# Retention and a softplus feed-forward layer: the decay of the queries moved to the outputs of the values, opening loads each into a buffer of its own, copies and rests on GpSimd

## The chip, the cores and the metric

The kernel runs on one core of one Trainium2 chip. The metric is the time of one execution on the device in microseconds (us). Below, PE is TensorE's matmul, PEld its weight load, DVE is VectorE, ACT is ScalarE, POOL is GpSimd and SP is SyncE, whose queue issues all transfers.

## What is computed

There are 8 sequences of 576 tokens with 8 heads of 64. Each head does retention, which is attention without a softmax, with scores that decay by a head's factor per token of distance; the result, 4608 tokens by 512, goes through a feed-forward layer with 2048 hidden units and a softplus between its two products.

```python
scores = scale * np.matmul(q, k.transpose(0, 1, 3, 2))
gamma = 1.0 - 2.0 ** (-5.0 - np.arange(H, dtype=np.float32))
Dmat = np.where(rel >= 0, gamma[:, None, None] ** rel[None, :, :], 0.0)
ret = scores * Dmat[None, :, :, :]
attn_out = np.matmul(ret, v)
...
h = x @ w_in
g = np.maximum(h, 0.0) + np.log1p(np.exp(-np.abs(h)))
return g @ w_out
```

The decay from token c to token r is split into two factors: gamma^(r+1), which goes with the query r, and gamma^-(c+1), which goes with the value c.

## The kernel before

**Retention in steps.** The 4608 tokens are 36 chunks of 128. A step m is half a chunk's heads, so there are 72 steps, two to a chunk. A step has up to 32 products of 64x64 (twice as many matmul records, since each is done in two passes): `scores` does 8 products of keys and queries into the score columns of a PSUM tile (L150) and then up to 8 products of keys and values, the sums from which a chunk's state is made (L155); `values` does 8 products of masked scores and values (L204) and up to 8 of states and queries (L214). In one place of the program, `scores` of step m and `values` of step m-1 stand together. `scores_out` masks the scores on DVE (L168), makes the running states u and s on DVE (L184, L193; L181, L182 and L191 at the start of a sequence) and sx, copies of states on the other half of the partitions, on POOL (L177) and DVE (L185), and scales s on POOL (L195). `values_out` writes the result of `values` into the tile xt as a head (a cast on ACT, L229) and a rest (a subtraction on DVE, L233).

**Scaling.** `scale_next` multiplies the queries of a step by the decay on POOL (L127, 128x384), in place, and from step 9 on the values too, also on POOL (L130, 128x256). The values of steps 0 to 8 are scaled on ACT in four pieces of 128x64 (L140, `scale_values`).

**The feed-forward layer in slots.** 512 tokens are a unit; there are 9 units and 16 slices of the hidden dimension, so 144 slots. Slot i does `hidden_mm(i)` (12 matmuls 128x512, L248), then ACT and DVE make the softplus (`logs`: Abs, Exp, Ln on ACT, L256 to L258; the sum on DVE, L262; the head g by a cast on ACT, L266, and the rest on DVE, L267), and PE goes on with `output_mm(i - 1)` (12 matmuls, L280). In odd slots, up to slot 127, one retention step stands ahead of `hidden_mm`: slot 1 has scores of step 9 and values of step 8, slot 3 those of 10 and 9, and so on, for the unit that comes next. At the end of a unit four results are copied out (ACT and DVE, L288 and L290) and stored.

**Weights.** The 32 weight pieces come as 64-bit floats in three staging buffers wst and are turned into two 32-bit parts while slots 0 to 14 run: L309 and L325 on ACT, L311, L317 and L330 on DVE, the last of these writing the part that `hidden_mm` of the next slot reads.

**The opening.** Ahead of slot 0, steps 0 to 8 run alone (`AHEAD` is 9), with `values` up to step 7, since `hidden_mm(0)` needs the whole xt of unit 0. The inputs of a step are 576 KB. The raw tiles have three buffers of their own and two that later belong to g, so the loads of steps 5 to 10 wait for buffers.

**What sets the order.** The program is scheduled by hand: each engine takes its instructions in the order in which they are written, and waits in its place for what an instruction needs.

Of the kernel before, what the change touches and what calls it, by code (L numbers as in the profile page):

```python
# [7 lines left out]
F32 = mybir.dt.float32  # L8
# [27 lines left out]
SMALL = 2 * QC  # L36
NCONST = NPAIR * QC + H + NPAIR
PIECE = 512
START_WEIGHTS = 2
OPENING = 5  # L40
# [18 lines left out]
def retention_softplus_ffn(ctx: ExitStack, tc, first, others, consts, w, out):  # L59
    nc = tc.nc  # L60

    const = ctx.enter_context(tc.tile_pool(name="const", bufs=1))
    wpool = ctx.enter_context(tc.tile_pool(name="wpool", bufs=1))
    xpool = ctx.enter_context(tc.tile_pool(name="xpool", bufs=2))
    att = ctx.enter_context(tc.tile_pool(name="att", bufs=2))
    moe = ctx.enter_context(tc.tile_pool(name="moe", bufs=2))
# [3 lines left out]
    ps_h = ctx.enter_context(tc.tile_pool(name="ps_h", bufs=2, space=PSUM))  # L70
    ps_att = ctx.enter_context(tc.tile_pool(name="ps_att", bufs=1, space=PSUM))
    rawp = ctx.enter_context(tc.tile_pool(name="rawp", bufs=3))
    weight_pools = ExitStack()
    wst = weight_pools.enter_context(tc.tile_pool(name="wst", bufs=WBUFS))
    later = {}

    consts_sb = const.tile([P, NCONST], F32, name="consts_sb")
    mask = const.tile([P, HC], F32, name="mask")

    decq = [consts_sb[:, n:n + SMALL].rearrange("p (s c) -> p s c", s=2) for n in (0, NCONST - SMALL)]  # L80
    vsc, gchp = consts_sb[:, SMALL:SMALL + H], consts_sb[:, SMALL + H:SMALL + H + NPAIR]


    ws = [wpool.tile([P, 2, 2 * PIECE], F32R, name=f"w{p}") for p in range(NF)]
# [17 lines left out]
    def load_step(m):  # L102

        pool, tag = (moe, "g") if m in (3, 4, 8) else (rawp, "rawp")
        r = pool.tile([P, RAW], F32, tag=tag, name=f"raw_{tag}")
        if m == 0:
            for to, at in ((consts_sb, slice(0, SMALL + H + NPAIR)), (r, slice(0, KQ)), (r, slice(KQ, RAW)),
                           (consts_sb, slice(NCONST - SMALL, NCONST))):
                nc.sync.dma_start(to[:, at], (first if to is r else consts)[:, at])
        else:  # L110
            nc.sync.dma_start(r, others[m - 1])
        kq, kv = r[:, 0:KQ], r[:, KQ:]
# [5 lines left out]
    scaled = [0]  # L118

    def scale_next():  # L120

        m = scaled[0]
        if m not in live:
            return
        scaled[0] += 1
        q = live[m]["q"]
        nc.gpsimd.tensor_mul(q, q, decq[m % 2])  # L127
        if m >= AHEAD:
            v, f = value_scale(m)
            nc.gpsimd.tensor_mul(v, v, f.unsqueeze(2).broadcast_to([P, 4, D]))  # L130
# [372 lines left out]
```

## Time and profile before

| what | value |
|---|---|
| time, median of 3 runs | 918.75 us (917.89 to 921.36) |
| the profiled execution's own time | 918.31 us |
| its span in the profile | 916.6 us |
| PE busy | 890.4 us, 97% |
| ACT busy | 442.1 us, 48% |
| DVE busy | 375.6 us, 41% |
| POOL busy | 165.6 us, 18% |
| mean granted PE clock | 0.991 |

The span is the profiled execution from its first to its last instruction; 1.7 us lie around it. A busy share is an average over three stages: the opening, the slots in which weights are still being turned into parts, and the rest. A row of the timeline has the start, the length, the engine, the line and the operation, out<-in by the program's names and, in brackets, how long the engine had been idle and what ended that.

### The profile page before, as it was taken

The page shows a single profiled execution, that of the slowest core. Times are in us where ns is not written, and L with a number is a line of the kernel's source. Part 1 is how long each engine was busy: PE and PEld are TensorE (multiplying, and loading weights), DVE is VectorE, ACT ScalarE, POOL GpSimd, SP SyncE. Part 2 cuts the span into 40 slices and gives each one's busy share as a digit, 9 for nine tenths or more (in the row PEclk, how much of TensorE's full clock was granted, in tenths as well). Part 3 has the DMA queues.
Part 4 walks back from the last instruction along what each step waited for, and adds up shares of the span by engine and source line. Part 5 has one row for each costly group of instructions (what it writes and reads, how often), then busy time and mean ns, then how long its engine had stood idle before and what let it go on. Part 6 is the DMA issues. An engine that isn't in the chain of part 4 may idle for free.

```text
span 916.6 us, 18132 instructions
## 1 busy us (share of the span) xinstructions
PE 890.4 (97%) x7830; PEld 725.7 (79%) x7830; DVE 375.6 (41%) x745; ACT 442.1 (48%) x775; POOL 165.6 (18%) x270
## 2 busy tenths in 40 slices
PE   6699999999999999999999999999999999999998
PEld 5477778888888888888888888888888888888886
DVE  4588884333423333333333333334333333332222
ACT  5577775444444454444544454445444544444444
POOL 5322121122121111111211222111211122100000
PEclk7899999999999999999999999999999999999999
DMA  8456652111211112111211121112111131001001
GB/s 289 179 189 210 201 176 76 53 52 53 99 52 53 52 38 89 53 53 52 99 53 52 36 89 53 52 54 98 53 53 45 36 98 53 27 1 46 1 1 46
DMA packets 20671, 70.24 MB, mean 77 GB/s; under 512 B 2288, under 2 KB 2544, under 8 KB 20592
## 3 DMA queue, kind: packets, MB, share of 16 engines
q1 hardware_dynamic: 20592, 69.09, 22.7%
q8 instruction: 61, 1.00, 0.5%
q14 instruction: 18, 0.15, 0.1%
HBM read 59.64 MB, written 9.44 MB: 75 GB/s over the span
## 4 chain that ended last, share of the span: by engine, by line
PE 90%; DVE 3%; ACT 3%; DMA 2%; POOL 1%; issue 0%; SPq 0%; POOLq 0%; DVEq 0%
PE h L248 43%; PE y L280 40%; PE bank L150 3%; PE bank L214 2%; PE bank L204 2%; PE bank L155 1%; DMA raw_g<-others 1%; DVE w L330 1%; DMA raw_rawp<-others 1%; DVE ab L262 1%; ACT ab L257 1%; ACT ab L258 1%; DMA wst<-w 1%; DVE wst L317 1%; ACT w L325 0%; ACT ab L256 0%
## 5 line engine op out<-in xcount | busy, mean ns | idle before, releaser
L248 PE MATMUL h<-xt,w 128*128 128x512 f32 (+1 forms) x1740 | 426.6, 394 | 8.7 <-DVE w L330 8.6
L280 PE MATMUL y<-w,g 128*128 128x512 f32 x1728 | 414.9, 389 | 0.0
L248 PEld LDWEIGHTS h<-xt,w 128*128 128x128 f32 x1740 | 320.6, 188 | 80.4 <-DVE w L330 11.9
L280 PEld LDWEIGHTS y<-w,g 128*128 128x128 f32 x1728 | 324.3, 188 | 67.3
L262 DVE SCALAR_TENSOR_TENSOR ab<-h,ab 128x512 f32<-128x512 f32 (+1 forms) x145 | 99.7, 688 | 410.1 <-ACT ab L258 410.1
L256 ACT ACTIVATE ab<-h 128x512 f32<-128x512 f32 (+1 forms) x145 | 86.3, 595 | 299.4 <-PE h L248 298.9
L267 DVE TENSOR_TENSOR g<-ab,g 128x512 fp32r<-128x512 f32 (+1 forms) x145 | 104.8, 723 | 90.9 <-ACT g L266 89.2
L266 ACT CAST g<-ab 128x512 fp32r<-128x512 f32 (+1 forms) x145 | 89.4, 617 | 101.0 <-DVE ab L262 99.9
L127 POOL TENSOR_TENSOR raw_rawp<-raw_rawp,consts_sb 128x384 f32<-128x384 f32 x69 | 72.1, 1045 | 198.8 <-DMA raw_rawp<-others 195.6
L195 POOL TENSOR_TENSOR s<-s,consts_sb 128x128 f32<-128x128 f32 x64 | 26.1, 408 | 417.8 <-DVE s L193 368.6
L258 ACT ACTIVATE ab<-ab 128x512 f32<-128x512 f32 (+1 forms) x145 | 91.2, 629 | 4.7
L257 ACT ACTIVATE ab<-ab 128x512 f32<-128x512 f32 (+1 forms) x145 | 91.2, 629 | 4.6
L130 POOL TENSOR_TENSOR raw_rawp<-raw_rawp,consts_sb 128x256 f32<-128x256 f32 x63 | 41.7, 661 | 0.0
L229 ACT CAST xt<-bank 128x256 fp32r<-128x256 f32 x68 | 25.4, 373 | 32.8 <-PE bank L214 32.8
L150 PEld LDWEIGHTS bank<-raw_rawp 64*64 64x64 f32 x1008 | 20.4, 133 | 22.2 <-issue 22.2
L214 PE MATMUL bank<-raw_rawp,sx 64*64 64x64 f32 x472 | 27.8, 221 | 4.1 <-POOL sx L177 4.1
L204 PE MATMUL bank<-a,raw_rawp 64*64 64x64 f32 x1056 | 30.1, 221 | 1.0 <-DVE xt L233 1.0
L233 DVE TENSOR_TENSOR xt<-bank,xt 128x256 fp32r<-128x256 f32 x68 | 28.3, 416 | 6.5 <-ACT xt L229 6.3
L168 DVE TENSOR_TENSOR a<-bank,mask 128x256 f32<-128x256 f32 x63 | 26.6, 423 | 9.6 <-ACT xt L229 9.6
L150 PE MATMUL bank<-raw_rawp 64*64 64x64 f32 x1008 | 29.1, 230 | 0.0
L177 POOL COPY sx<-s 64x128 f32<-64x128 f32 x64 | 24.8, 388 | 8.8 <-PE bank L214 4.8
L155 PE MATMUL bank<-raw_rawp 64*64 64x64 f32 x888 | 25.9, 218 | 0.0
(74 smaller groups left out, 412.7 us busy)
## 6 DMA issues: line engine op xcount, KB each, us to landing
raw_rawp<-others SPq DMA_DIRECT2D x68, 576.0 KB, 4.0
wst<-w SPq DMA_DIRECT2D x32, 512.0 KB, 3.7
out<-osb SPq DMA_DIRECT2D x36, 256.0 KB, 2.4
raw_g<-others SPq DMA_DIRECT2D x3, 576.0 KB, 8.8
raw_rawp<-first SPq DMA_DIRECT2D x1, 320.0 KB, 3.4
raw_rawp<-first SPq DMA_DIRECT2D x1, 256.0 KB, 4.7
consts_sb<-consts SPq DMA_DIRECT2D x1, 198.0 KB, 2.5
consts_sb<-consts SPq DMA_DIRECT2D x1, 192.0 KB, 4.9
```

Source lines behind the costliest of these rows:

```text
L127: nc.gpsimd.tensor_mul(q, q, decq[m % 2])
L150: nc.tensor.matmul(bank[rows[t], h, SCOLS][:, part[s]], L["k"][rows[h], s, part[t]], L["q"][rows[h], s, part[t]], start=True, stop=True, s ...
L204: nc.tensor.matmul(o[t][rows[h], part[s]], L["v"][rows[t], s, rows[h]], L["a"][rows[t], h, s], start=(s == 0), stop=L["states"][t] is None ...
L214: nc.tensor.matmul(o[t][rows[h], part[s]], lhs[rows[t], s], rhs, start=False, stop=True, skip_group_check=True)
L248: nc.tensor.matmul(h, ws[p][:, a, kt * P:(kt + 1) * P], xt[:, b, kt, cols], start=(n == 0), stop=(n == 3 * NKT - 1))
L256: nc.scalar.activation(ab, h, AF.Abs)
L257: nc.scalar.activation(ab, ab, AF.Exp, scale=-1.0)
L258: nc.scalar.activation(ab, ab, AF.Ln, bias=1.0)
L262: nc.vector.scalar_tensor_tensor(ab, h, 0.0, ab, op0=ALU.max, op1=ALU.add)
L266: nc.scalar.copy(g[:, HI], ab)
L267: nc.vector.tensor_sub(g[:, LO], ab, g[:, HI].bitcast(F32))
L280: nc.tensor.matmul(y, g[:, a, at:at + P], ws[p][:, b, PIECE:], start=(p == 0 and n == 0), stop=(p == NF - 1 and n == 2))
```

## The change

- The queries are no longer scaled. The decay multiplies the output of `values` instead: `values_out` does a DVE multiplication of 128x256 into a new tile x, then the cast to the head on ACT, and then the rest, on POOL (for step 7, on DVE).
- The values of all steps are scaled on ACT (`scale_values`, four pieces). In the slots, this stands in even slots behind the cast of g: `scale_values(AHEAD + i // 2)` in slot i, for the step whose products stand at the head of slot i + 1.
- `scores` is cut in two. The sums are now `sums`, and PE does them behind `values`. `states_out` is the second half of the former `scores_out`, and comes behind `values_out`.
- The second copy into sx moves from DVE to POOL and reads u rather than PSUM.
- The inputs of steps 0 to 10 each have a buffer of their own, in the space of the second half of the weights, and those of steps 0 to 8 are issued at the start, with weight piece 0 behind step 3 and pieces 1 and 2 behind step 8. The first transfers carry the constants with them; a second copy of the constants is loaded later. From step 11 on, the raw tiles have two buffers rather than three.
- The opening matmuls that have nothing to do (`OPENING`) go from 5 to 3. PSUM tiles of the opening are arranged anew, and pools change sides.

The diff, cut to its core:

```diff
-OPENING = 5
+OPENING = 3
+NOPEN = AHEAD + 2
...
     def load_step(m):
-        pool, tag = (moe, "g") if m in (3, 4, 8) else (rawp, "rawp")
-        r = pool.tile([P, RAW], F32, tag=tag, name=f"raw_{tag}")
         if m == 0:
...
+            if m < NOPEN:
+                r = openp.tile([P, RAW], F32, name=f"raw{m}")
+            else:
+                r = rawp.tile([P, RAW], F32, tag="rawp", name="rawp")
             nc.sync.dma_start(r, others[m - 1])
...
-    def scale_next():
...
-        nc.gpsimd.tensor_mul(q, q, decq[m % 2])
-        if m >= AHEAD:
-            v, f = value_scale(m)
-            nc.gpsimd.tensor_mul(v, v, f.unsqueeze(2).broadcast_to([P, 4, D]))
...
     def scale_values(m):
-        if m < AHEAD:
-            v, f = value_scale(m)
-            for n in range(4):
-                nc.scalar.activation(v[:, n], v[:, n], AF.Copy, scale=f[:, n:n + 1])
+        if m >= NSTEP:
+            return
+        v = live[m]["v"].rearrange("p s (h d) -> p (s h) d", h=2)
+        f = constant[0][0][:, 4 * (m % 2):4 * (m % 2) + 4]
+        for n in range(4):
+            nc.scalar.activation(v[:, n], v[:, n], AF.Copy, scale=f[:, n:n + 1])
...
+    def sums(m):
...
                 if follows if t else start != HC:
-                    nc.tensor.matmul(bank[rows[h], t, TCOLS][:, part[s]], L["kp"][rows[t], s, rows[h]],
+                    nc.tensor.matmul(L["bank"][rows[h], t, TCOLS][:, part[s]], L["kp"][rows[t], s, rows[h]],
                                      L["v"][rows[t], s, rows[h]], start=True, stop=True, skip_group_check=True)
...
-                nc.vector.tensor_add(sx[rows[1]], sums[0][rows[0]], before[rows[0]])
+            nc.gpsimd.tensor_copy(sx[rows[1]], between[rows[0]])
...
-        for head, _, src in todo:
-            nc.scalar.copy(head, src)
...
-                nc.vector.tensor_sub(rest, src, head.bitcast(F32))
...
+        x = att.tile([P, 2, C], F32, tag="x", name="x")
+        nc.vector.tensor_mul(x.rearrange("p s (t c) -> p s t c", t=2),
+                             bank[:, :, VCOLS].rearrange("p t (s c) -> p s t c", s=2),
+                             constant[0][2][:, pr:pr + 2].rearrange("p s (t c) -> p s t c", t=2))
+        nc.scalar.copy(hi, x)
+        rest.tensor_sub(lo, x, hi.bitcast(F32))
...
+    first_weights = {3: (0,), 8: (1, 2)}
...
-    for m in range(5):
+    for m in range(AHEAD):
         load_step(m)
-        if m == 3:
-            load_weight(0)
+        for n in first_weights.get(m, ()):
+            load_weight(n)
...
     for i in range(NSLOT):
         m = AHEAD + (i - 1) // 2
         if i % 2 and m <= NSTEP:
...
-            scores(m, both)
-            values(m - 1, [both[:, n] for n in range(2)])
-            rest = values_out(m - 1, both)
+            scores(m, bank)
+            values(m - 1, bank)
+            sums(m)
             scores_out(m)
-            rest()
-            load_next()
-            scale_next()
+            values_out(m - 1, bank, nc.gpsimd)
+            states_out(m)
+            if NOPEN <= m + 1 < NSTEP:
+                load_step(m + 1)
...
         weight_cd(n)
         gs[i] = [softplus_split(ab)]
+        if i % 2 == 0:
+            scale_values(AHEAD + i // 2)
         weight_a(n + 1)
```

In the opening, step m of the loop now writes: scores of m, values of m-1, sums of m, `scores_out(m)`, `values_out(m - 1)`, `scale_values(m + 1)`, `states_out(m)`.

The three places in the program of which the prediction speaks, in each engine's own order. First ACT, over one odd and one even slot late in the program, before: L256 to L258 are the logs of a slot, L266 the cast of g, L229 the head of the retention result.

```order
L229 CAST xt_2703<-bank 128x2x128
L256 ACTIVATE ab<-h 128x512
L257 ACTIVATE ab<-ab 128x512
L258 ACTIVATE ab<-ab 128x512
L266 CAST g<-ab 128x512
L256 ACTIVATE ab<-h 128x512
L257 ACTIVATE ab<-ab 128x512
L258 ACTIVATE ab<-ab 128x512
L266 CAST g<-ab 128x512
L229 CAST xt_2703<-bank 128x2x128
```

And of the change, where L265 to L267 are the logs, L275 the cast of g, L147 the scaling of the values and L242 the head:

```order
L242 CAST xt_2772<-x 128x2x128
L265 ACTIVATE ab<-h 128x512
L266 ACTIVATE ab<-ab 128x512
L267 ACTIVATE ab<-ab 128x512
L275 CAST g<-ab 128x512
L265 ACTIVATE ab<-h 128x512
L266 ACTIVATE ab<-ab 128x512
L267 ACTIVATE ab<-ab 128x512
L275 CAST g<-ab 128x512
L147 ACTIVATE rawp<-rawp,consts_sb 128x64 x4
L242 CAST xt_2772<-x 128x2x128
```

Four scalings now stand behind the even slot's cast of g, ahead of the next step's head.

Second, PE at the head of an odd slot, before: the last output products of the slot ahead (L280), scores (L150), sums (L155), values (L204 and L214), and the hidden products (L248).

```order
L280 MATMUL y_1817<-w_96,g 128x512 x3
L150 MATMUL bank<-raw_rawp 64x64 x8
L155 MATMUL bank<-raw_rawp 64x64 x8
L204 MATMUL bank<-a,raw_rawp 64x64 x8
L214 MATMUL bank<-raw_rawp,s 64x64
L214 MATMUL bank<-raw_rawp,sx 64x64 x2
L214 MATMUL bank<-raw_rawp,u 64x64
L214 MATMUL bank<-raw_rawp,s 64x64
L214 MATMUL bank<-raw_rawp,sx 64x64 x2
L214 MATMUL bank<-raw_rawp,u 64x64
L248 MATMUL h<-xt_662,w_98 128x512 x12
```

And of the change, with L155 the scores, L218 and L229 the values, L168 the sums and L257 the hidden products:

```order
L155 MATMUL bank<-rawp 64x64 x8
L218 MATMUL bank<-a,rawp 64x64 x8
L229 MATMUL bank<-rawp,s 64x64
L229 MATMUL bank<-rawp,sx 64x64 x2
L229 MATMUL bank<-rawp,u 64x64
L229 MATMUL bank<-rawp,s 64x64
L229 MATMUL bank<-rawp,sx 64x64 x2
L229 MATMUL bank<-rawp,u 64x64
L168 MATMUL bank<-rawp 64x64 x8
L257 MATMUL h<-xt_1816,w_970 128x512 x12
```

The sums went from second to last place, directly ahead of the hidden products.

Third, POOL at the end of the opening, before: the scaling of queries (L127) and, from step 9 on, of values (L130), the copy into sx (L177) and the scaling of s (L195).

```order
L127 TENSOR_TENSOR raw_g<-raw_g,consts_sb 128x384
L177 COPY sx<-s 64x128
L195 TENSOR_TENSOR s<-s,consts_sb 128x128
L127 TENSOR_TENSOR raw_rawp<-raw_rawp,consts_sb 128x384
L130 TENSOR_TENSOR raw_rawp<-raw_rawp,consts_sb 128x256
L177 COPY sx<-s 64x128
L195 TENSOR_TENSOR s<-s,consts_sb 128x128
```

And of the change, with L243 the rest, L193 and L200 the two copies into sx and L210 the scaling of s:

```order
L243 TENSOR_TENSOR xt_203<-x,xt_203 128x2x128
L193 COPY sx<-s 64x128
L200 COPY sx<-u 64x128
L210 TENSOR_TENSOR s<-s,part_91 128x128
L243 TENSOR_TENSOR xt_203<-x,xt_203 128x2x128
L193 COPY sx<-s 64x128
L200 COPY sx<-u 64x128
L210 TENSOR_TENSOR s<-s,part_91 128x128
```

No instruction there reads a raw tile any more; each step has a rest and a second copy instead.

More of the change, by code (lines that the diff above doesn't have):

```diff
@@ L431, in retention_softplus_ffn @@
             weight_pools.close()
-            later["osb"] = ctx.enter_context(tc.tile_pool(name="osb", bufs=4))
+            later["osb"] = ctx.enter_context(tc.tile_pool(name="osb", bufs=4, side="right"))
         if i > 0:
@@ L485 @@
     gchp = np.broadcast_to(gch.reshape(NPAIR, 2, 1), (NPAIR, 2, D)).reshape(NPAIR, P).T
[L486 removed]
     arrays = {
[L488 removed]
+        "first": np.concatenate([kq[0], vsc, gchp, kv[0], decp], axis=1).astype(np.float32),
         "others": np.concatenate([kq[1:], kv[1:]], axis=2),
[L490 removed]
+        "consts": np.concatenate([vsc, gchp, decp], axis=1).astype(np.float32),
         "w": np.stack([w_in, w_out], axis=1),
```

180 lines of the change are left out of this document (84 added, 96 removed).

## The prediction

> **What bounds the kernel now.** I read the page first, for the share of each engine and the chain that ended last.
>
> ```profile
> PE 890.4 (97%) x7830; PEld 725.7 (79%) x7830; DVE 375.6 (41%) x745; ACT 442.1 (48%) x775; POOL 165.6 (18%) x270
> ...
> PE 90%; DVE 3%; ACT 3%; DMA 2%; POOL 1%; issue 0%; SPq 0%; POOLq 0%; DVEq 0%
> ```
>
> PE is busy 97% of the span and is 90% of the chain. What is left for a change to win lies at the start; what it can lose is any wait that it puts into PE's order. The busy times by stage say where.
>
> ```profile
> 68.00:101.00 33.00, 30.79 (x254) 24.19 (x248) 29.05 (x55) 24.48 (x43) 7.77 (x11) 1.00 0.60 203
> ...
> 135.00:440.00 305.00, 305.00 (x2713) 248.85 (x2714) 111.68 (x227) 137.74 (x235) 55.98 (x92) 1.00 0.19 60
> ```
>
> The columns are the length, then busy time of PE, PEld, DVE, ACT and POOL, then the granted clock, the DMA share and GB/s. From 135 us on PE has no gap at all. While weights are made (68 to 101) DVE is busy 29.05 of 33 us and PE waits a little. So there are three stages: the opening up to about 33 us, the weight slots up to about 135, and a full PE.
>
> Then the timeline of one period of the last stage, two slots.
>
> ```profile
> 438.69 0.46 PE L150 MATMUL bank<-raw_rawp 64*64 64x64 f32 x16
> 438.77 0.62 ACT L266 CAST g<-ab 128x512 fp32r<-128x512 f32 x1 [0.76 <-DVE ab L262]
> 438.98 0.41 PE L155 MATMUL bank<-raw_rawp 64*64 64x64 f32 x16
> ...
> 439.29 1.07 ACT L288 COPY osb<-y 128x512 f32<-128x512 f32 x2
> ...
> 439.79 3.02 PE L248 MATMUL h<-xt,w 128*128 128x512 f32 x12
> ...
> 448.28 0.60 ACT L256 ACTIVATE ab<-h 128x512 f32<-128x512 f32 x1 [2.14 <-PE h L248]
> ...
> 450.89 0.46 PE L150 MATMUL bank<-raw_rawp 64*64 64x64 f32 x16
> 450.97 0.62 ACT L266 CAST g<-ab 128x512 fp32r<-128x512 f32 x1 [0.76 <-DVE ab L262]
> ```
>
> A period is 450.89 - 438.69 = 12.20 us. The line to hold on to is the even slot's cast of g: it starts 0.08 us after the retention step's scores start on PE, in both periods shown. That distance is no accident. The cast follows from the end of `hidden_mm` by way of the three logs (448.28 to 450.97), and the scores follow from the same end by the 12 output products. Neither depends on anything else.
>
> **The sums behind the scaling of the values.** This is the step that decides. The change puts four ACT scalings behind that cast, and the products that read the scaled values stand at the head of the very next slot. What four such scalings take, and how fast PE answers, the opening shows.
>
> ```profile
> 6.52 1.06 ACT L140 ACTIVATE raw_rawp<-raw_rawp,consts_sb 128x64 f32<-128x64 f32 x4 [4.44 <-DMA raw_rawp<-first]
> 6.92 0.92 PEld L155 LDWEIGHTS pair<-raw_rawp 64*64 64x64 f32 x16 [0.68 <-ACT raw_rawp L140]
> ```
>
> Four take 1.06 us, and the groups give the length of one:
>
> ```profile
> L140 ACT ACTIVATE raw_rawp<-raw_rawp,consts_sb 128x64 f32<-128x64 f32 x24 | 6.4, 341 | 6.7 <-DMA raw_rawp<-first 4.4 <-DMA raw_rawp<-others 2.3
> ...
> L150 PE MATMUL bank<-raw_rawp 64*64 64x64 f32 x1008 | 29.1, 230 | 0.0
> ```
>
> The first ends at 6.52 + 0.34 = 6.86, and PE starts 0.06 us later. The 1008 records of scores are 16 to a step, so 63 steps (9 to 71) lie in slots.
>
> Now the period again, with the change. ACT's next instruction begins 439.29 - 438.77 = 0.52 us after the cast begins, so the fourth scaling ends at 438.77 + 0.52 + 1.06 = 440.35, and PE sees it at 440.41. The 64 records of a full step, from 438.69 to 439.79, take 1.10 us: about 0.23 for each 16 and 0.17 until the hidden products start. With the sums in last place they come up at 438.69 + 3 x 0.23 = 439.38 and would be done in time for 439.79; instead they wait for the pieces one by one. Behind the fourth piece 6 of their 16 records are left (0.09), then 0.17: the hidden products start at 440.67. That is **0.88 us later, in every period**.
>
> Nothing covers this. PE takes its matmuls in order, so all of the hidden products wait behind the sums, and the period is a loop: the next even slot's cast is 12.2 us after this one in PE's own work, and moves with PE. In the last stage it costs 55 steps (17 to 71) x 0.88 = 48.4 us. As bounds for a step I take 0.75 (half a scaling less than the rows give) and 1.00.
>
> **The weight slots.** Seven steps, 10 to 16, lie there. These rows of the chain show how slots follow one another, and a row of the groups the mean of a weight part.
>
> ```profile
> 46.68 1.26 DVE w L330
> ...
> 57.79 0.61 ACT ab L256
> ...
> 61.25 3.01 PE h L248 x12
> ```
>
> ```profile
> L330 DVE TENSOR_TENSOR w<-wst,w 128x512 fp32r<-128x512 f32 x32 | 23.9, 747 | 3.1 <-ACT w L325 3.0
> ```
>
> From the end of one `hidden_mm` (57.79) to the start of the next (61.25) it is 3.46 us by way of logs, sum and weight part; the other slot of the pair is bound by PE. The two parts stand in series, so the 0.88 us adds. Beside it, the weight's first ACT instruction now stands 1.06 us later behind the scalings, and the head of the retention result waits on ACT for its DVE product; I put 0.2 on that. On the other side POOL's scaling is gone, and with it perhaps the long weight parts: this one takes 1.26 us against the 0.747 mean of the group, and 0.3 a pair is my estimate from that difference of 0.5.
>
> I take 0.8 a step, 5.6 us, with 0.3 and 1.3 as bounds. Slot 1 is apart.
>
> ```profile
> 24.15 5.43 DMA raw_rawp<-others
> ...
> 29.74 0.99 POOL raw_rawp L127
> ...
> 31.36 0.30 POOL sx L177
> ...
> 31.70 0.59 PE bank L214 x11
> ...
> 33.26 4.46 PE h L248 x12
> 37.74 0.61 ACT ab L256
> ...
> 41.04 3.05 PE h L248 x12
> ```
>
> ```profile
> 40.47 0.62 ACT L266 CAST g<-ab 128x512 fp32r<-128x512 f32 x1 [0.27 <-DVE ab L262]
> ```
>
> From 37.74 to `hidden_mm(1)` it was 3.30 us. With the sums of step 9 in front it is 2.73 to the cast, then 0.52 + 1.06 + 0.06 + 0.09 + 0.17, together 4.63: 1.3 us more.
>
> **The opening.** The rows above show a fault that the change removes. POOL stood waiting at the query scaling of a step whose load landed only at 29.58, and the copy sx for step 7, behind it in POOL's order, came at 31.36, so `hidden_mm(0)` started at 33.26. With all loads issued at the start and no scaling on POOL this wait is gone. What is late next is the loop of a step, which the new rest on POOL lengthens.
>
> ```profile
> L168 DVE TENSOR_TENSOR a<-bank,mask 128x256 f32<-128x256 f32 x63 | 26.6, 423 | 9.6 <-ACT xt L229 9.6
> L229 ACT CAST xt<-bank 128x256 fp32r<-128x256 f32 x68 | 25.4, 373 | 32.8 <-PE bank L214 32.8
> L130 POOL TENSOR_TENSOR raw_rawp<-raw_rawp,consts_sb 128x256 f32<-128x256 f32 x63 | 41.7, 661 | 0.0
> ```
>
> From the end of `values` it goes through the DVE product (0.42, as L168), the cast (0.37), the rest on POOL (0.66, as L130), two copies into sx (0.30 each, as at 31.36), 0.3 on PE and six answers of 0.06: 2.7 us a step. Bounds are 2.2, if the copies do not wait for the rest, and 3.1.
>
> ```profile
> 9.51 1.06 ACT L140 ACTIVATE raw_rawp<-raw_rawp,consts_sb 128x64 f32<-128x64 f32 x4 [1.93 <-DMA raw_rawp<-others]
> ```
>
> ```profile
> 25.00:30.00 5.00, 1.01 (x32) 0.74 (x32) 1.88 (x7) 1.03 (x5) 1.54 (x4) 0.96 0.92 335
> 30.00:35.00 5.00, 3.29 (x42) 2.85 (x43) 1.99 (x5) 1.52 (x3) 4.65 (x9) 0.50 0.02 6
> ```
>
> ```profile
> 31.70 0.37 PE L214 MATMUL bank<-raw_rawp,sx 64*64 64x64 f32 x2 [3.68 <-POOL sx L177]
> ```
>
> Step 1's inputs were there at 9.5, with slightly more bytes ahead of them than now, so `values` of step 0 ends at about 9.6 and that of step 7 at 9.6 + 7 x 2.7 = 28.5. A product and a cast (0.9 with answers) make it 29.4 for `hidden_mm(0)`. The loads are hidden by that: 5958 KB up to step 8, at the 335 GB/s of the row from 25 to 30, are 18.2 us from about 2.5.
>
> `hidden_mm(0)` took 4.46 us at a granted clock of 0.50, after PE had done 1.01 us of work in five; a warm one takes 3.02. I take 3.5 for it, so its end is 32.9 against 37.72, a gain of 4.8 us, with 1.5 and 8 as bounds. The Trainium skill ("TensorE: Matmul & The Clock Gate", What's actually happening) says that the clock halves after an idle window of about 3.4 us; the row agrees, the wait ahead having been 3.68 us. By that rule the shorter waits of the change would leave `hidden_mm(0)` at 3.02, and the whole 0.5 us below my sum.
>
> ```profile
> raw_rawp<-others SPq DMA_DIRECT2D x68, 576.0 KB, 4.0
> ```
>
> Without cost are the moved copy (DVE is idle over half the time in the last stage), the rest on POOL there (0.66 us in 12 us, for a tile that is read at the earliest a slot later), the two raw buffers (a load takes 4.0 us at the median and has most of a 12.2 us period) and the three opening matmuls. If one of these covers were gone it would cost at most its own length, below 0.7 us a step.
>
> **The sum.** 48.4 + 5.6 + 1.3 - 4.8 = 50.5 us, on the profiled execution's own 918.3: 968.8 us. That execution stands 0.4 us below the median of 918.75, which is inside the spread of the runs.
>
> **The rivals.** A, not slower: the scaling is done when the sums come. From the cast's start to PE's answer there would have to be no more than 0.76 us, where the rows give 1.64, or PE would have to reach the step 0.88 us later. It holds only if ACT's scalings run ahead of the cast, and the order puts them behind it. Then only the opening and the relief in the weight slots (7 x 0.3) are left: 918.3 - 4.8 - 2.1 = 911.4 us. Chance 0.04.
>
> B, also not slower: PE runs on past the waiting sums with the hidden products. Against it speaks the wait up to 31.70: behind the products that waited for sx stood scores which needed nothing, and the chain has `hidden_mm` only behind all of them. The time is that of A, 911.4. The Trainium skill ("TensorE: Matmul & The Clock Gate", Step-by-step: what each phase is for) says the same, that only weight loads are pulled ahead and matmuls stay in program order. Chance 0.02.
>
> C, slower still: in the weight slots DVE, at 29.05 of 33 us, becomes the bound because its weight instructions wait on an ACT queue which is 1.06 us later. Each of 7 pairs then costs about 2.5 us rather than 0.8, and the opening gives back only 1.5: 968.8 + 11.9 + 3.3 = 984 us. Chance 0.06.
>
> D: the short waits make the clock fall. If `hidden_mm` behind each wait ran as at 33.26, 4.46 rather than 3.02, it would cost 62 x 1.44 = 89 us more, 1058 us. Against it: the weight stage has waits of about 1 us ahead of `hidden_mm` and a clock of 1.00. The Trainium skill names such a mode in "TensorE: Matmul & The Clock Gate", A second HAM failure mode: psum-queue depth-cycling; this trace does not show it. Chance 0.02.
>
> **How the numbers follow.** The forecast has 0.86, and the predicted time is its sum, 968.8. Its low end is 918.3 + 55 x 0.75 + 7 x 0.3 + 1.3 - 8 = 955; its high end 918.3 + 55 x 1.00 + 7 x 1.3 + 1.3 - 1.5 = 982. Taken together the terms will hardly all go one way, so 955 to 982 holds more than 8 in 10 of it, and what is left out, the rivals with it, is less than 2 in 10. Half a per cent, 4.6 us, is about what a measurement of this kernel can tell from no change. Faster by more than that: A and B, 0.06, of which 0.01 may fall within it: 0.05. Within it: that and 0.01 for an error in the forecast, 0.02. Slower: 0.93.
>
> **What would show it.** If right, the waits list has PE waiting for ACT's scalings about 63 times with 0.7 to 1.0 us each, the period of two slots in the last stage is 13.1 us rather than 12.2, PE is no longer without gaps from 135 us on, and `hidden_mm(0)` starts at about 29. It is wrong if the hidden products start within 1.2 us of the scores in the last stage, if the clock there falls below 0.95, or if the weight slots take more than 10 us longer than they did.

## The result and the profile after

The changed kernel takes 994.09 us (median of 4 runs, 993.76 to 995.94) against 918.58 for the kernel before (4 runs, 917.89 to 921.36). The ratio is 1.082, with a 95% interval of 1.0804 to 1.0835. The direction is as forecast; the time is 25 us over the forecast and 12 us over the top of its range. The profiled execution, 995.94 us with a span of 994.2, is the longest of the four, 1.85 us over the median.

The page after, its busy line and its chain:

```profile
PE 971.3 (98%) x7826; PEld 767.6 (77%) x7826; DVE 348.3 (35%) x678; ACT 504.1 (51%) x1023; POOL 122.7 (12%) x270
...
PE 89%; ACT 5%; DVE 2%; issue 2%; POOL 1%; DMA 1%; SPq 0%; POOLq 0%
```

PE has four records fewer and 81 us more busy time. So the loss is hardly a gap on PE: it lies inside what counts as busy. The stages say the same (columns as in the prediction):

```profile
68.00:101.00 33.00, 31.34 (x242) 23.99 (x241) 25.40 (x48) 25.80 (x50) 6.46 (x10) 1.00 0.55 185
135.00:440.00 305.00, 304.45 (x2455) 240.30 (x2456) 101.13 (x197) 152.82 (x311) 37.27 (x82) 1.00 0.19 61
440.00:813.00 373.00, 373.00 (x3074) 294.80 (x3064) 115.66 (x227) 182.03 (x377) 45.42 (x104) 1.00 0.17 57
```

From 440 to 813 us PE is shown as busy for all of 373.00 us at a clock of 1.00. The count tells what the busy time hides: in the 305 us from 135 on there are 2455 matmuls, and before there were 2713.

One period of the last stage, in the timeline after: L275 is the cast of g, L147 the scaling of the values, L155 the scores, L168 the sums, L257 the hidden products.

```profile
492.71 0.62 ACT L275 CAST g<-ab 128x512 fp32r<-128x512 f32 x1 [0.76 <-DVE ab L271]
...
492.72 0.46 PE L155 MATMUL bank<-rawp 64*64 64x64 f32 x16
...
493.24 1.06 ACT L147 ACTIVATE rawp<-rawp,consts_sb 128x64 f32<-128x64 f32 x4
...
493.63 1.05 PE L168 MATMUL bank<-rawp 64*64 64x64 f32 x16
...
494.62 3.06 PE L257 MATMUL h<-xt,w 128*128 128x512 f32 x12
...
506.02 0.46 PE L155 MATMUL bank<-rawp 64*64 64x64 f32 x16
```

The sums take 1.05 us where 16 such records took 0.41, because they wait for the four pieces of the values one after the other. From the scores to the hidden products it is 494.62 - 492.72 = 1.90 us, before it was 1.10: **0.80 us a period**. The period itself is 506.02 - 492.72 = 13.30 us in this place, and 13.268 in the mean of 56 (hidden products 15 to 127), against 12.182 in the same mean before. That is 1.086 more, so 0.29 us a period is something else.

What else, the end of the program shows best, where there is no retention any more. First before, then after, PE's rows over a few slots:

```profile
820.02 2.88 PE L280 MATMUL y<-w,g 128*128 128x512 f32 x12
822.74 2.88 PE L248 MATMUL h<-xt,w 128*128 128x512 f32 x12
825.46 2.88 PE L280 MATMUL y<-w,g 128*128 128x512 f32 x12
828.18 2.88 PE L248 MATMUL h<-xt,w 128*128 128x512 f32 x12
```

```profile
897.76 2.96 PE L257 MATMUL h<-xt,w 128*128 128x512 f32 x12
900.56 2.96 PE L289 MATMUL y<-w,g 128*128 128x512 f32 x12
903.35 2.97 PE L257 MATMUL h<-xt,w 128*128 128x512 f32 x12
906.16 2.97 PE L289 MATMUL y<-w,g 128*128 128x512 f32 x12
```

Twelve products that wait for nothing go from 2.72 to 2.80 us. The diff leaves these products untouched, and the clock is 1.00 in both. Between the starts of two neighbours it was 226.7 ns in the mean, and is 234.0 (hidden) and 233.8 (output). All big products run 3% slower; four such groups a period, at 0.08 each, account for the 0.29.

The opening went the other way than forecast. Timeline after, of one step: L193 and L200 are the copies into sx, L229 the products that read sx, L177 the masked scores, L239 the product with the decay, L242 the head, L243 the rest.

```profile
15.00 0.29 POOL L193 COPY sx<-s 64x128 f32<-64x128 f32 x1
15.34 0.71 PE L229 MATMUL bank<-raw,sx 64*64 64x64 f32 x3 [1.02 <-POOL sx L193]
15.34 0.29 POOL L200 COPY sx<-u 64x128 f32<-64x128 f32 x1
...
16.85 0.42 DVE L177 TENSOR_TENSOR a<-pair,mask 128x256 f32<-128x256 f32 x1 [2.63 <-PE pair L168]
17.19 0.41 DVE L239 TENSOR_TENSOR x<-bank,part 128x256 f32<-128x256 f32 x1
...
17.64 0.40 ACT L242 CAST xt<-x 128x256 fp32r<-128x256 f32 x1 [2.54 <-DVE x L239]
...
18.12 0.92 POOL L243 TENSOR_TENSOR xt<-x,xt 128x256 fp32r<-128x256 f32 x1 [2.01 <-ACT xt L242]
...
19.11 0.29 POOL L193 COPY sx<-s 64x128 f32<-64x128 f32 x1
```

The loop is the one that I named, from a copy to the next, but it takes 19.11 - 15.00 = 4.11 us rather than 2.7 (the other full steps take 3.9 to 4.4). The piece that I put at 0.3 on PE is 17.19 - 15.34 = 1.85: after the copy PE does the products with states and then the sums, DVE waits for these sums with L177, and the decay product L239 stands behind L177. PE does all this at half clock, and so it does the first two calls of `hidden_mm`:

```profile
15.00:20.00 5.00, 3.34 (x74) 2.85 (x78) 1.58 (x5) 2.02 (x7) 2.65 (x7) 0.50 1.01 405
...
37.00:43.00 6.00, 6.00 (x36) 4.52 (x29) 4.05 (x9) 2.27 (x4) 0.58 (x2) 0.51 0.04 12
```

```profile
37.84 5.36 PE L257 MATMUL h<-xt,w 128*128 128x512 f32 x12
...
46.83 1.19 PE L168 MATMUL bank<-raw 64*64 64x64 f32 x8 [2.78 <-ACT raw L147]
47.95 5.42 PE L257 MATMUL h<-xt,w 128*128 128x512 f32 x12
...
56.71 3.07 PE L257 MATMUL h<-xt,w 128*128 128x512 f32 x12 [0.54 <-DVE w L339]
```

`hidden_mm(0)` starts at 37.84 (before 33.19) and takes over 5.3 us, and so does `hidden_mm(1)`, behind a wait of 2.78 us for the scaling of step 9; before it took 3.05. `hidden_mm(1)` starts 4.75 us after the end of `hidden_mm(0)` (43.20 to 47.95), close to the 4.63 of the forecast; that it would be cold was not in it.

The spans, stage by stage, by the starts of the hidden products (number 2 at 56.71 against 47.98, 15 at 149.03 against 134.96, 127 at 892.05 against 817.16):

| stage | before, us | after, us | difference | forecast |
|---|---|---|---|---|
| up to hidden product 2 | 47.98 | 56.71 | +8.7 | -4.8 + 1.3 |
| 2 to 15, weight slots | 86.97 | 92.32 | +5.4 | +5.6 |
| 15 to 127, waits of the sums, 56 x 0.80 | | | +44.6 | +48.4 |
| 15 to 127, slower products, 56 x 0.29 | | | +16.2 | none |
| 127 to the end | 99.45 | 102.18 | +2.7 | none |
| span | 916.6 | 994.2 | +77.6 | +50.5 |

### The profile page after: what moved, and what is told of

Read it like the earlier page. It is cut to its first block, busy times and chain, and to the rows that moved or that the text cites. A ratio compares the mean times of both kernels' runs of the same rounds, so it can differ in the third digit from the quotient of the medians.

```text
span 994.2 us, 18273 instructions
## 1 busy us (share of the span) xinstructions
PE 971.3 (98%) x7826; PEld 767.6 (77%) x7826; DVE 348.3 (35%) x678; ACT 504.1 (51%) x1023; POOL 122.7 (12%) x270
## 4 chain that ended last, share of the span: by engine, by line
PE 89%; ACT 5%; DVE 2%; issue 2%; POOL 1%; DMA 1%; SPq 0%; POOLq 0%
PE h L257 41%; PE y L289 37%; PE bank L168 6%; PE bank L155 2%; PE bank L229 1%; PE bank L218 1%; DVE ab L271 1%; ACT ab L267 1%; ACT ab L266 1%; ACT ab L265 1%; ACT wst L318 1%; POOL xt L243 1%; DMA raw<-others 1%; ACT rawp L147 0%; DVE w L339 0%
## 5 line engine op out<-in xcount | busy, mean ns | idle before, releaser
L257 PE MATMUL h<-xt,w 128*128 128x512 f32 (+1 forms) x1740 | 438.8, 401 | 3.8 <-DVE w L339 3.8
L289 PE MATMUL y<-w,g 128*128 128x512 f32 x1728 | 426.7, 396 | 0.0
L257 PEld LDWEIGHTS h<-xt,w 128*128 128x128 f32 x1740 | 322.9, 190 | 84.3 <-DVE w L339 6.9
L265 ACT ACTIVATE ab<-h 128x512 f32<-128x512 f32 (+1 forms) x145 | 86.3, 595 | 269.1 <-PE h L257 269.1
L243 POOL TENSOR_TENSOR xt<-x,xt 128x256 fp32r<-128x256 f32 x71 | 54.6, 769 | 750.2 <-ACT xt L242 666.4
L275 ACT CAST g<-ab 128x512 fp32r<-128x512 f32 (+1 forms) x145 | 89.3, 616 | 101.4 <-DVE ab L271 100.2
L267 ACT ACTIVATE ab<-ab 128x512 f32<-128x512 f32 (+1 forms) x145 | 91.4, 630 | 4.6
L266 ACT ACTIVATE ab<-ab 128x512 f32<-128x512 f32 (+1 forms) x145 | 91.2, 629 | 4.6
L242 ACT CAST xt<-x 128x256 fp32r<-128x256 f32 x72 | 29.3, 406 | 94.7 <-DVE x L239 94.7
L147 ACT ACTIVATE rawp<-rawp,consts_sb 128x64 f32<-128x64 f32 x244 | 64.6, 335 | 0.0
L168 PE MATMUL bank<-rawp 64*64 64x64 f32 x864 | 64.1, 242 | 0.0
L168 PEld LDWEIGHTS bank<-rawp 64*64 64x64 f32 x864 | 47.1, 131 | 15.8
L177 DVE TENSOR_TENSOR a<-bank,mask 128x256 f32<-128x256 f32 x63 | 26.6, 422 | 32.8 <-PE bank L168 32.8
L155 PEld LDWEIGHTS bank<-rawp 64*64 64x64 f32 x976 | 19.8, 133 | 22.4 <-issue 22.4
L155 PE MATMUL bank<-rawp 64*64 64x64 f32 x976 | 28.2, 230 | 0.0
L239 DVE TENSOR_TENSOR x<-bank,consts_sb 128x256 f32<-128x256 f32 x64 | 26.5, 414 | 0.0
L339 DVE TENSOR_TENSOR w<-wst,w 128x512 fp32r<-128x512 f32 x32 | 22.4, 701 | 9.5 <-ACT w L334 9.5
L218 PE MATMUL bank<-a,rawp 64*64 64x64 f32 x976 | 25.2, 218 | 0.0
L210 POOL TENSOR_TENSOR s<-s,consts_sb 128x128 f32<-128x128 f32 x55 | 24.4, 443 | 4.4
```

Source lines behind the costliest of these rows:

```text
L147: nc.scalar.activation(v[:, n], v[:, n], AF.Copy, scale=f[:, n:n + 1])
L155: nc.tensor.matmul(bank[rows[t], h, SCOLS][:, part[s]], L["k"][rows[h], s, part[t]], L["q"][rows[h], s, part[t]], start=True, stop=True, s ...
L168: nc.tensor.matmul(L["bank"][rows[h], t, TCOLS][:, part[s]], L["kp"][rows[t], s, rows[h]], L["v"][rows[t], s, rows[h]], start=True, stop=T ...
L243: rest.tensor_sub(lo, x, hi.bitcast(F32))
L257: nc.tensor.matmul(h, ws[p][:, a, kt * P:(kt + 1) * P], xt[:, b, kt, cols], start=(n == 0), stop=(n == 3 * NKT - 1))
L265: nc.scalar.activation(ab, h, AF.Abs)
```

## The experiments

My theory after the result: (1) the sums wait for ACT, 0.80 us a period; (2) the big products are slower because the pools changed sides, and so the tiles have other addresses; (3) the opening is held up by a loop over the rests on POOL, at half clock. The rivals: for (1), that PE's waits come from the new order on PE and not from ACT; for (2), that the slower products come from the waits, from other traffic to SBUF, or from the place of one tile alone; for (3), that the loads or the cold clock set the pace.

In the built programs a tile's start address within a partition can be read. What I compare is its remainder by 512 for the weights w, for x (xt) and for g. The pieces of these tiles that a product reads start at multiples of 512 bytes within the tile, so the remainder is that of the operand too. The mean spacing is taken over neighbours of the same call in the last part of the program, 85 to 20 us from its end. A ratio is to runs of the kernel before beside that kernel's own; their medians go from 918.58 to 920.04.

| kernel | w / xt / g | spacing of hidden / output products, ns | time, us | ratio to before (95%) |
|---|---|---|---|---|
| before | 448 / 448 / 448 | 226.7 / 226.7 | 918.58 | 1 |
| after | 128 / 480 / 480 | 234.0 / 233.8 | 994.09 | 1.082 (1.0804 to 1.0835) |
| `align` | 128 / 448 / 448 | 232.0 / 233.5 | 990.17 | 1.0751 (1.0729 to 1.0774) |
| `early` | 128 / 480 / 480 | 234.0 / 233.8 | 951.35 | 1.0334 (1.0313 to 1.0355) |
| `align_early` | 128 / 448 / 448 | 232.0 / 233.4 | 946.62 | 1.0284 (1.0259 to 1.0309) |
| `before_shift` | 448 / 480 / 480 | 233.2 / 233.5 | 941.58 | 1.0226 (1.0205 to 1.0247) |
| `before_all32` | 480 / 480 / 480 | 226.7 / 226.7 | 919.69 | 1.0006 (0.9991 to 1.0022) |
| `half512_early` | 128 / 384 / 384 | 226.7 / 226.7 | 931.0 | 1.0144 (1.0122 to 1.0167) |
| `same512_early` | 128 / 128 / 128 | 226.6 / 226.6 | 931.81 | 1.0146 (1.0126 to 1.0166) |
| `diff128_early` | 128 / 256 / 256 | 233.4 / 233.4 | 948.9 | 1.0324 (1.0305 to 1.0343) |
| `xt_only_early` | 128 / 128 / 480 | 227.5 / 234.3 | 944.27 | 1.0273 (1.0253 to 1.0292) |
| `best1` | 128 / 128 / 128 | 226.6 / 226.6 | 922.25 | 1.0036 (1.002 to 1.0051) |
| `best2` | 128 / 128 / 128 | 226.6 / 226.6 | 915.7 | 0.9963 (0.9949 to 0.9977) |
| `best2_warm` | 128 / 128 / 128 | 226.6 / 226.6 | 917.1 | 0.998 (0.9969 to 0.999) |

**Does the wait come from ACT's place in the order?** `early` is the changed kernel with the four scalings between Ln and the sum of the softplus, one softplus ahead of the cast of g:

```diff
+        if i % 2 == 0:
+            scale_values(AHEAD + i // 2)
         softplus(h, ab)
         weight_cd(n)
         gs[i] = [softplus_split(ab)]
-        if i % 2 == 0:
-            scale_values(AHEAD + i // 2)
```

> The change with the four scalings of the values moved in even slots from behind the cast of g to behind the logs, so ahead of the cast. Theory 1, the wait of the sums: they are scaled 0.7 us before PE comes to them, the wait of 0.80 us is gone in 56 periods of the last stage and mostly in the weight slots; the period goes from 13.27 to 12.5 and the time from 994 to about 946. Theory 2, ACT's time is merely moved: the cast comes 0.3 us later, g with it, and PE waits in the output products instead; over 980. The products stay at 2.80 us for 12 either way.

Its period in the last stage is 12.471 us, 0.80 less than after, and the kernel is 43 us faster than after. The timeline of one period:

```profile
484.31 1.05 ACT L147 ACTIVATE rawp<-rawp,consts_sb 128x64 f32<-128x64 f32 x4
...
485.18 0.46 PE L155 MATMUL bank<-rawp 64*64 64x64 f32 x16
485.26 0.60 ACT L275 CAST g<-ab 128x512 fp32r<-128x512 f32 x1
...
485.93 0.41 PE L168 MATMUL bank<-rawp 64*64 64x64 f32 x16
...
486.27 3.06 PE L257 MATMUL h<-xt,w 128*128 128x512 f32 x12
```

The scalings are done at 485.36, the sums take 0.41 us again, and from scores to hidden products it is 1.09. PE's order is the same as after, so it was ACT's. What is left, 12.471 against 12.182, is the slower products. The time is 5 us over the 946 that I expected, and this lies in the weight slots: from hidden product 2 to 15 they take 94.09 us (after 92.32, before 86.97), although the sums do not wait there either (0.41 us). There the scalings now hold up the cast of a weight piece on ACT, its rest on DVE, and through them PE, which waits 10.2 us for weight parts (after 3.8, before 6.2). The same 5 to 6 us are missing in `same512_early`, `half512_early` and `best1`, whose weight slots take 93.7 to 93.9 us.

**Is it the address?** `align` puts 32 bytes between the start of the right side and its pools, `align_early` does that in `early`, and `before_shift` puts 32 bytes into the kernel before, behind the weights' pool, so that only the constants and w keep their place (the edit shown is that of `align`):

```diff
+    pad = ctx.enter_context(tc.tile_pool(name="pad", bufs=1, side="right"))
+    pad.tile([P, 8], F32, name="pad0")
     rawp, moe, att = right("rawp", 2), right("moe", 2), right("att", 2)
```

> The change with one tile of 32 bytes put first on the right side, so that all tiles there (xt, g, ab, the raw tiles) start at a multiple of 64 bytes, as all did before; in the change they start 32 bytes off. Theory 1, the address: a product that reads an operand 32 bytes off takes 233 ns rather than 227, so 12 products go back from 2.80 to 2.72 us, the tail behind slot 127 from 102.2 to 99.4, the period of the last stage from 13.27 to 12.98, and the time from 994 to about 974. Theory 2, the 233 ns come from the new place of the PSUM tiles or the weights, or from the load of the other engines: nothing changes, 994.

> Both edits, the 32 bytes and the earlier scaling. If the two costs are separate, they add: period 12.2 as before the change, tail 99.4, and what is left of the loss is the opening and slots 0 to 2, 8.7 us, with some of it given back in the weight slots: about 926. If both were one (products slow because PE waits, or the reverse), this is no better than the better of the two.

> The kernel before, with one tile of 32 bytes between the weights and xt, so that xt, g, ab, the raw tiles and the staging tiles start 32 bytes off a multiple of 64, and nothing else. Theory 1, the address: 12 products take 2.80 us, the period of the last stage goes from 12.18 to 12.48, the tail from 99.4 to 102.2, and the time from 918.6 to about 939. Theory 2, the change's other new places or its load on ACT and POOL make products slow: no change, 918.6.

`before_shift` settles that it is the address: not an instruction differs, and 32 bytes cost 21.5 us (941.58 against 920.04 beside it). `align` gains 3.9 us on after and `align_early` 4.7 on `early`, where I expected 20: a start that is a multiple of 64 does not bring the 226.7 back. Then it might be the remainder itself, or the difference between the two operands of a product. `before_all32` moves all three by 32 bytes (the pad ahead of all pools), `same512_early` and `half512_early` are `early` with pads of 352 and 96 bytes.

> The kernel before with 32 bytes put ahead of everything, so that the weights, xt and g all move by 32 and stay equal by 512 (480). Theory 1, the difference between the operands: 226.7 ns and no change, about 919. Theory 2, the remainder itself: 233 ns and about 941, as where only xt and g moved by 32.

> The change with the earlier scaling, and 352 bytes put first on the right side, so that the weights, xt and g all start at 128 above a multiple of 512 bytes. Before the change all three stand at 448; in the change the weights stand at 128 and xt and g at 480; with 32 bytes less at 128 and 448, which left the products slow. Theory 1, the difference between the two operands of a product: at equal remainders by 512 the products take 226.7 ns again, the tail 99.4 us, the period 12.18, and the time is about 926. Theory 2, the remainder itself, 448 being a good one: products stay at 233 and the time at about 947.

> As the kernel with equal remainders, but 96 bytes put first: the weights at 128, xt and g at 384, a difference of 256. If what counts is the difference by 64, 128 or 256 the products take 226.7 ns and the time is about 926; if it is the difference by 512 they take about 233 and the time is about 946. Theory 2, the remainder itself, gives 946 too.

`before_all32` is as fast as before at odd multiples of 32, so it is not the remainder: it is the difference. At differences of 0 and 256 the products are back at 226.7 ns, and the period of the last stage at 12.182 us, exactly that before. PE's rows at the end of `same512_early`:

```profile
874.04 2.88 PE L259 MATMUL h<-xt,w 128*128 128x512 f32 x12
876.76 2.88 PE L291 MATMUL y<-w,g 128*128 128x512 f32 x12
879.48 2.88 PE L259 MATMUL h<-xt,w 128*128 128x512 f32 x12
```

From `early` to `same512_early` the time falls from 951.35 to 931.81 us, by 19.5. Two more kernels ask for the rule: `diff128_early` (a pad of 224 bytes) and `xt_only_early` (352 bytes behind x's pool, so that x is in step with w and g is not).

```diff
     rawp, moe, att = right("rawp", 2), right("moe", 2), right("att", 2)
+    pad = ctx.enter_context(tc.tile_pool(name="pad", bufs=1, side="right"))
+    pad.tile([P, 88], F32, name="pad0")
     xpool, const = right("xpool", 2), right("const", 1)
```

> The changed kernel with the early scalings and a pad of 224 bytes, so that the starts of x and g stand 128 bytes (by 512) from those of the weights. If a difference of 128 is as good as 0 and 256: 226.7 ns between products, a period of 12.18, about 931 us. If only multiples of 256 are: 232 to 234 ns, a period of 12.4 to 12.5, about 949 us. In between, the cost would grow with the distance from a multiple of 256: 229 to 231 ns, about 940 us.

> The changed kernel with the early scalings and the pad of 352 bytes put behind x's pool, so that x starts at the remainder of the weights and g stays 352 away. If each product pays for the difference of its own two operands: 226.7 ns between the hidden products and 233.8 between the output products, a period of about 12.33, 940 us. If one pair out of step slows all products: both at 233 to 234, 950 us. If it is g's place, or what lies near it, that counts for both: also 233 to 234 for the hidden products.

A difference of 128 is as slow as the others (233.4 ns). In `xt_only_early` each kind of product pays for its own two operands:

```profile
885.48 2.89 PE L259 MATMUL h<-xt,w 128*128 128x512 f32 x12
888.21 2.97 PE L291 MATMUL y<-w,g 128*128 128x512 f32 x12
891.02 2.89 PE L259 MATMUL h<-xt,w 128*128 128x512 f32 x12
893.75 2.97 PE L291 MATMUL y<-w,g 128*128 128x512 f32 x12
```

The hidden products take 2.73 us (885.48 to 888.21), the output products 2.81 (888.21 to 891.02), side by side in one program. The time, 944.27, is above the 940 that I expected: the period is 12.381 us, not 12.33. What was tried agrees with this rule: full speed where the starts of the two operands differ by a multiple of 256 bytes, and about 3% lost at 32, 64, 96 and 128 by 256. Why the hardware does so, none of these runs shows.

**The opening.** `best1` is `same512_early` with the copies into sx ahead of the rest on POOL:

```diff
-        if 0 < m < AHEAD - 1:
-            values_out(m - 1, bank, nc.gpsimd)
         if m < AHEAD - 1:
             scale_values(m + 1)
         states_out(m)
+        if 0 < m < AHEAD - 1:
+            values_out(m - 1, bank, nc.gpsimd)
```

> The kernel with equal remainders and earlier scaling, and in the opening the states ahead of the output of the values: the copies into sx no longer stand on POOL behind the rest, which waits for the cast. Theory 1, the loop of a step in the opening (sums, masked scores, product, cast, rest, two copies, values, 4.1 us): without the product, the cast and the rest in the loop it is about 2.6 us, hidden_mm(0) starts at about 27 rather than 37, and the time is some 9 us below the kernel without this, about 917. Theory 2, the opening is bound by the landing of its loads: it starts no earlier than 35, less than 2 us gained.

`hidden_mm(0)` starts at 28.68 us, 9.6 earlier than in `same512_early` (38.26), so the place of the rest on POOL made the loop long, and not the landing of the loads. But the first two calls are still cold, 5.13 and 5.49 us, and hidden product 2 starts at 46.88, 1.1 us before that of the kernel before. The weight slots (hidden products 2 to 15) take 93.7 us there, before 86.97. `best2` keeps that opening and the pad, takes the scaling from step 9 on off ACT and gives it to POOL, as before:

```diff
+        nc.gpsimd.tensor_mul(v, v, f.unsqueeze(2).broadcast_to([P, 4, D]))
...
             if NOPEN <= m + 1 < NSTEP:
                 load_step(m + 1)
+                scale_pool(m + 1)
...
-        if i % 2 == 0:
-            scale_values(AHEAD + i // 2)
```

> The changed kernel with the operands 352 bytes lower, so that the starts of weights, x and g leave the same remainder by 512, the state copies of the opening ahead of the rests on GpSimd, and the values of steps 9 on scaled by one GpSimd product behind the load of the step, as the kernel before does, instead of four ACT instructions in the even slots. If the loss that stays in the version with the early scalings (922.25 us; its hidden products 2 to 15 take 93.7 us, before 87.0) is ACT's four scalings standing ahead of the weights' casts: hidden products 2 to 15 in 87 to 89 us, a period of 12.18 in the last stage, about 916 us. If it is the new casts and rests of x in those slots: 92 to 94 us for products 2 to 15 and 921 to 923 us. If GpSimd's product holds up the copies behind it: a period above 12.3 and over 927 us.

It takes 915.7 us, faster than the kernel before by 0.37% (ratio 0.9949 to 0.9977). The weight slots take 88.8 us, so most of the loss there was ACT's scalings ahead of the weights' casts: PE waits 11.5 us for weight parts in `best1`'s and 7.2 in `best2`'s. The other 1.8 us over the kernel before remain unexplained. The period is 12.182. One step on POOL in `best2` (L203 and L210 are the copies, L253 the rest), and the stretch around the start of `hidden_mm(0)`, at 27.82:

```profile
14.09 0.29 POOL L203 COPY sx<-s 64x128 f32<-64x128 f32 x1
14.43 0.29 POOL L210 COPY sx<-u 64x128 f32<-64x128 f32 x1
...
15.50 0.73 POOL L253 TENSOR_TENSOR xt<-x,xt 128x256 fp32r<-128x256 f32 x1 [0.30 <-ACT xt L252]
16.29 0.29 POOL L203 COPY sx<-s 64x128 f32<-64x128 f32 x1
```

```profile
25.00:33.00 8.00, 7.18 (x116) 5.72 (x116) 5.97 (x13) 4.27 (x9) 4.46 (x9) 1.00 0.36 118
```

This step is 16.29 - 14.09 = 2.20 us; the others take 2.2 to 3.6. The last row shows a clock of 1.00, where `best1` shows 0.50 from 25 to 28 us in an opening that is written alike, and from this I took it that the clock had stayed up in `best2`. So `best2_warm` asks whether idle products keep it up:

```diff
         sums(m)
+        if m > 2:
+            for n in range(2):
+                nc.tensor.matmul(pair[:, 0, 2 * C:3 * C], fill[:, 0:P], fill[:, 0:C], start=True, stop=True,
+                                 skip_group_check=True)
         scores_out(m)
```

> The same kernel (operands in step, state copies first in the opening, values scaled by GpSimd from step 9 on) with two more idle products of 128x128 on PE in each opening step from the fourth on, which nothing reads. If the first two hidden_mm calls take 5.1 and 5.5 us because PE had been idle for too much of the steps before them (granted clock 0.50 in 25 to 29 us of the version with early scalings): they take 2.7 to 3.3 us each, and hidden_mm(2) starts 3 to 4 us earlier, against a start of hidden_mm(0) that the idle products move by at most 1 us. If the clock goes by something else than the idle time of PE: both calls still take over 5 us, and the time is that without the idle products or up to 3 us longer.

That reading of the clock was wrong. In `best2`'s trace the record of the clock begins only at 29.68 us, and a stretch without a record is shown as 1.00. The products tell more. These are PE's rows in `best2`, then in `best2_warm`, whose record has 1.00 from 9.38 to 19.62 us and 0.50 from there to 26.45:

```profile
17.08 0.71 PE L228 MATMUL bank<-a,raw 64*64 64x64 f32 x16
...
27.82 3.89 PE L267 MATMUL h<-xt,w 128*128 128x512 f32 x12
```

```profile
16.85 0.46 PE L228 MATMUL bank<-a,raw 64*64 64x64 f32 x16
...
21.17 0.37 PE L178 MATMUL pair<-raw 64*64 64x64 f32 x1 [3.10 <-issue]
...
23.21 0.71 PE L228 MATMUL bank<-a,raw 64*64 64x64 f32 x16
...
30.79 3.01 PE L267 MATMUL h<-xt,w 128*128 128x512 f32 x12
```

At 1.00 the 16 products take 0.46 us, at 0.50 they take 0.71, and so they do in `best2` at 17.08. Its opening ran at half clock up to 29.7 us, that of `same512_early` up to 40.1, and that of `best1` except from 19.6 to 23.1. So it was the order of the loop, and not the clock, that brought `hidden_mm(0)` forward, by 9.6 us in `best1`.

The idle products did not make the kernel faster: 917.1 us, 1.4 over `best2`, and the single times of the two overlap. The clock was up for part of the opening, and `hidden_mm(0)` took 3.01 us, but it started at 30.79, 3.0 later than in `best2`, and `hidden_mm(1)` still took 4.39. In its profile PE stood for 3.10 us before 21.17 for nothing that the profile shows; `best1` has such a wait of 1.88 us before 21.53 and `best2` one of 1.88 us before 20.83, at half clock. What that one waits for stays open, and so does whether the idle products raised the clock, since each kernel has one profile.

## Why the prediction was wrong, point by point

- **The wait of the sums: right.** The rivals A and B, in which it does not come, are out. The size was 0.80 and not 0.88 us. I had the cast start 0.08 us after the scores; it starts 0.01 before them (492.71 and 492.72). The 12 output products that lead up to the scores take 0.08 longer and the logs do not, which accounts for it. In 56 periods that is 44.6 us for my 48.4.
- **The products' own time: the step that is missing.** My sum took the products over at their length before, since the diff left them alone. But the diff says that pools change sides, and I did not ask what the addresses do to PE. 16.2 us in the last stage and 2.7 behind it are more than two thirds of the 27 us by which the span's sum failed; `same512_early` gives 19.5 for the whole program. None of my rivals had it, and the sign that I named (a clock below 0.95) could not show it: the clock is 1.00.
- **The opening: wrong in sign.** I put `hidden_mm(0)`'s end 4.8 us earlier, and it came 5.5 later. Two numbers failed. The loop of a step had "0.3 on PE" between copy and DVE, where there are 1.85 us, as L177 waits for the sums and the decay product stands behind it; and the clock. I had reckoned with 3.5 us for `hidden_mm(0)`, and both first calls took over 5.3. The loop is the larger: `hidden_mm(0)` starts 8.4 us after the 29.4 of the forecast and takes 1.9 longer than I put. How much of the 1.85 us is itself the half clock, no run shows, since none has this loop at full clock. The bound "if the copies do not wait for the rest", 2.2 us a step, is what the shortest steps of `best2` take, 2.20; the longest takes 3.6.
- **The clock rule.** I had used the idle window of about 3.4 us of the Trainium skill ("TensorE: Matmul & The Clock Gate", What's actually happening) for the thought that shorter waits would leave the clock up. Here the rows speak against it: from 8 to 38 us no gap on PE is over 1.5 us, and the granted clock is 0.50 in each stretch from 10 to 37. Nor did the kernel before bear the rule out as well as I thought: the record of its clock goes to 0.50 at 19.35 us behind a wait of only 1.70, and at 29.59, 1.57 us into the wait of 3.68. The same section of the Trainium skill says that the clock comes up after a window of sustained busy time; PE at 3.34 of 5 us, in pieces, did not lift it here.
- **The weight slots: right in the size**, 5.4 us for 5.6, and in part by luck. Seven waits of 0.80 are 5.6 us, and PE's waits for weight parts fell from 6.2 to 3.8, so 0.34 a pair for my 0.3. But 26 groups of slower products, at 0.08 each by my estimate 2.1 us, stand where I had put 0.2 a pair on ACT. Slot 1 is right as well (4.75 us for 4.63), apart from the cold product behind it. Rival C did not come: the weight slots are only 5.4 us longer. Rival D did not either: the clock is 1.00 behind the short waits of the last stage.
- **What was free: right.** The moved copy, the rest on POOL and two raw buffers cost nothing in the last stage, or `same512_early` would not have the 12.182 us before.
- **What would show it.** The period is 13.27 us for 13.1. The waits list shows no 63 waits: PE's only long wait for the scalings in it is the one in slot 1, since the others fall within a group of matmuls whose records, 0.22 to 0.27 us long, come 0.24 apart, and count as busy. For the same reason PE shows no gaps. Both signs were badly chosen; the period was the good one.

## What to carry to other kernels

An edit that moves pools can change the speed of instructions that it does not touch. Compare the start addresses of a matmul's two operands before and after (here 3% of all big products hung on their difference by 256 bytes), and look at the spacing of products that wait for nothing. And put what a consumer needs on its engine ahead of the work that ends together with the consumer's own start: four short scalings cost 43 us behind a cast, and nothing in the last stage ahead of it. Where PE is shown as fully busy, count its records per us: short waits inside a group of matmuls and slower products show there, not in the busy time. And check a clock of the profile against the length of like products: where its record has not begun, the view says 1.00.

## What the runs showed of the hardware

- A 128x512 product starts 226.7 ns after its neighbour when the starts of its two operands in SBUF differ by a multiple of 256 bytes (0 and 256 by 512 were tried), and 232 to 234 ns after it otherwise (32, 320, 352 and 128 by 512). The remainder itself does not count, and each product goes by its own pair.
- PE at about two thirds busy in short pieces, without a gap over 1.5 us, stayed at a granted clock of 0.50 for 27 us (the changed kernel, 10 to 37 us).
- A record of a 64x64 product lasts 0.31 us at a granted clock of 0.50 and 0.22 at 1.00, and neighbouring 128x512 products start 427 ns apart at 0.50.
